# Another order of all steps in a fused attention and channel-mix kernel, batch 0's first token half first

## The chip, the cores and the metric

The kernel runs on one core of a Trainium2 chip. The metric is the device time of one execution in microseconds. All times below are microseconds unless marked ns.

The engines are called as the profile calls them: PE is TensorE (PEld its weight loads), DVE is VectorE, ACT is ScalarE, POOL is GpSimd, SP is SyncE. Each takes its own list of instructions in order and waits for semaphores that other engines or transfers raise.

## The reference

Attention over 32 memory slots for each of 8 batches and 8 heads, 576 tokens and 64 columns a head; its output, with the heads side by side, goes through a token-shifted gated channel mix of width 512 and inner width 1024.

```python
a = phi - np.max(phi, axis=2, keepdims=True)
a = np.exp(a)
a = a / (np.sum(a, axis=2, keepdims=True) + 1e-09)
k_m = np.einsum('bhsm,bhsd->bhmd', a, k)
v_m = np.einsum('bhsm,bhsd->bhmd', a, v)
scores = scale * np.matmul(q, k_m.transpose(0, 1, 3, 2))
...
attn = np.exp(scores)
attn = attn / (np.sum(attn, axis=-1, keepdims=True) + 1e-09)
return np.matmul(attn, v_m).astype(np.float32)
...
x_prev = np.concatenate([np.zeros((B, 1, D), dtype=np.float32), x[:, :-1, :]], axis=1)
xk = mu_k * x + (1.0 - mu_k) * x_prev
xr = mu_r * x + (1.0 - mu_r) * x_prev
k = np.maximum(xk @ w_k, 0.0)
v = k * k @ w_v
r = 1.0 / (1.0 + np.exp(-(xr @ w_r)))
return (r * v).astype(np.float32)
```

## The kernel before

Nothing in this kernel is scheduled by a tool at build time. `PLAN` is a table of words, and the last loop of the kernel issues the steps that the words name, one after the other. Since each engine takes its instructions in the order in which they were issued, the order of the words is the order on every engine. A word reads `who:step@banks/engine`. `who` is a batch (`0:`, `1:`), a stage of the channel mix (`c0:` keys of batch 0, `g:` gates, `o:` outputs, `r:`, `t:` and `s:` evictions of keys, of gates, and squares, `x:` left-over tokens), `p:` a load and `b:` unread matmuls. The digits behind `@` say which of the eight PSUM banks the step writes, and `/a` or `/d` whether ACT or DVE does the copy. Many steps come in two or three words: the first issues the matmuls, a later one reads their result.

The steps of a batch's attention: `exp` (L292) exponentiates phi; `kv`, `k`, `v`, `kg`, `vg` (L312) multiply it with k or v (`kvps`); `z` (L322, L326) makes the reciprocal of its sum (`rz`); `nk` or `h` (L337 on ACT, L339 on DVE) normalizes k (`kbd`); `tk` (L361, L365) transposes it (`ktps`, `kmT`); `q0` and `q1` (L381) transpose q on DVE; `s` (L395) makes the scores (`scps`); `es` (L409, L413) exponentiates them.

For batch 0, which has nothing ahead of it to hide behind, the softmax goes over two parts of the attention positions, 0 to 319 and 320 to 575: `l` (L420, L425) takes the row sum by a matmul and its logarithm, `r` (L430) the reciprocal by an exponential, `y` (L458) weighs. Then `nk0`, `nk1`, `nr0` and `nr1` (L521, `vm`) scale V by the mix factors, `mk` and `mr` (L355, `mxps`) mix tokens and values in one go, `u` (L545) unloads the mix to `x0T`, and `c0:` (L599) multiplies it with `wk`. All of these exist for tokens 0 to 255 (`mk0`, `mr0`, `c0:..a`) and 256 to 575 (`mk1`, `mr1`, `c0:..b`). The first part reads attention positions 0 to 319 alone, the second one reads positions of both parts.

For batches 1 to 7 the softmax sum is folded on DVE (`fe` L435, `fs` L441 and L442, `fo` L447) and `w` (L458) weighs. `nv` (L346, L348) normalizes V, `vt` (L463, L468) transposes it, `vm` (L473, tile `vM`) scales the transpose. `G` (L492) multiplies both into the weights, `E` (L498) copies the result, `D` (L501) takes a difference, `c1:` to `c7:` (L617, L621, L625) make the keys from it, `g:` (L679, L683, L687) the gates, and `o:` (L760 on PE, L771 on DVE) multiplies the squares with `wv` and applies the gate; then the tile is stored. The outputs of batch 0 come as two halves of the columns (`o:00a`, `o:00b`), those of the last tile, `o:71`, as pieces of 352 (`a`, stored by ACT) and 160 columns (`b`, stored by SP).

Loads of weights and of the batches stand in POOL's list; phi and k of batch 0 are loaded by ACT. A load waits on POOL for the buffer it fills, and for the eighth load ahead of it to have landed. Unread matmuls (`keep_busy`, L259) multiply a tile of zeros; nothing reads what they write. Ten of them (`WARM`) come first.

## Time and profile before

| | |
|---|---|
| three executions | 189.34, 189.7, 189.8 us; median 189.7 |
| the profiled execution, span from first to last instruction | 187.8 us; no time of its own is given beside it |
| PE, DVE, ACT, POOL busy | 181.2, 153.9, 152.0, 30.2 us |
| from 20 to 180 us | PE busy 160.0 us |
| 0 to 10, 10 to 20 us | PE busy 8.8 and 8.2 us, unread matmuls among it |
| share of the 16 DMA engines' time | 0.8 or more from 5 to 112 us |

In the profile a busy PE is not PE at its peak, since matmuls are pipelined and their ends are modelled. A row of the timeline gives the start, the time from the first start to the last end, the engine, the line, output and inputs, and the count; in brackets the idle time ahead of it and what ended that. Rows of one engine can overlap a little.

### The profile page before, as it was taken

To read this page: it belongs to the slowest core of one execution; us is meant where nothing else is said; L and a number is where in the kernel's file an instruction comes from. 1 tells how busy PE (TensorE), PEld (TensorE's weight loads), DVE (VectorE), ACT (ScalarE), POOL (GpSimd) and SP (SyncE) were. 2 spreads that over 40 slices of the span, in tenths; PEclk is the share of its full clock that TensorE was granted. 3 is DMA by queue.
4 is the path that set the end of the run, shared out by engine and by line. 5 is a ranking of instruction groups with operands and counts; after the bars stand their busy time and mean duration, and the time that the engine had idled before them with its cause. 6 is when DMAs were issued, how large, how long until landed. Compare 5 with 4: busy or idle time off the path is not lost.

```text
span 187.8 us, 6010 instructions
## 1 busy us (share of the span) xinstructions
PE 181.2 (96%) x2483; PEld 103.2 (55%) x2483; DVE 153.9 (82%) x328; ACT 151.9 (81%) x368; POOL 30.2 (16%) x46
## 2 busy tenths in 40 slices
PE   7979999999999999999999999999999999999992
PEld 2544566677644575556544655556545653465441
DVE  2334574899989999999999899999989999889441
ACT  2537889889999999999999889958999678775900
POOL 5943531060303040140032000000000010000000
PEclk9999999999999999999999999999999999999999
DMA  5999999999999999899989995114202224242054
GB/s 188 280 203 220 251 207 205 266 208 234 308 208 210 275 292 255 160 220 224 223 163 237 234 278 197 28 59 113 56 0 59 58 59 113 56 108 63 0 139 140
DMA packets 24923, 31.91 MB, mean 170 GB/s; under 512 B 1880, under 2 KB 19040, under 8 KB 24896
## 3 DMA queue, kind: packets, MB, share of 16 engines
q0 software_dynamic: 17936, 20.45, 59.0%
q1 hardware_dynamic: 5664, 9.00, 17.2%
q10 hardware_dynamic: 1296, 2.08, 3.3%
q8 instruction: 19, 0.31, 0.7%
q14 instruction: 8, 0.07, 0.1%
HBM read 38.28 MB, written 9.44 MB: 254 GB/s over the span
## 4 chain that ended last, share of the span: by engine, by line
PE 90%; DMA 4%; DVE 2%; issue 1%; ACT 1%; POOL 0%; POOLq 0%; DVEq 0%
PE pv L760 34%; PE pk L617 8%; PE pk L625 8%; PE pb L625 7%; PE gps L492 6%; PE pk L599 4%; DMA q<-in_q_dram 4%; PE pr L687 3%; PE pb L687 3%; PE pr L679 3%; PE kvps L312 3%; PE pr L709 2%; PE pr L666 2%; PE scps L395 2%; PE idle L259 1%
## 5 line engine op out<-in xcount | busy, mean ns | idle before, releaser
L760 PE MATMUL pv<-wv,sq 128*128 128x512 bf16 (+3 forms) x296 | 60.5, 350 | 0.0
L760 PEld LDWEIGHTS <-sq 128*128 128x128 bf16 x296 | 27.7, 98 | 24.9 <-issue 2.8
L498 ACT CAST G<-gps 128x512 bf16<-128x512 f32 x67 | 36.2, 629 | 1.2 <-PE gps L492 1.2
L771 DVE SCALAR_TENSOR_TENSOR o<-sg,pv 128x512 f32<-128x512 f32 (+3 forms) x41 | 24.9, 613 | 7.5 <-PE pv L760 5.1
L625 PEld LDWEIGHTS <-G 128*128 128x128 bf16 x224 | 21.4, 98 | 8.5 <-issue 0.7
L583 ACT ACTIVATE rl<-pk 128x288 bf16<-128x288 f32 (+2 forms) x49 | 20.0, 420 | 4.5 <-PE pk L625 3.9
L625 PE MATMUL pk<-diff,G 128*128 128x288 bf16 x112 | 22.9, 286 | 0.0
L625 PE MATMUL pb<-diff,G 128*128 128x288 bf16 x112 | 22.9, 286 | 0.0
L617 PE MATMUL pk<-atn,G 128*128 128x288 bf16 x112 | 20.8, 287 | 0.0
L621 ACT COPY pb<-pk 128x288 f32<-128x288 f32 x41 | 16.4, 410 | 5.1 <-PE pk L617 3.5
L591 DVE TENSOR_TENSOR sq<-rl 128x576 bf16<-128x576 bf16 (+2 forms) x46 | 18.3, 420 | 1.0 <-ACT rl L583 0.5
L583 ACT ACTIVATE rl<-pb 128x288 bf16<-128x288 f32 x40 | 16.2, 427 | 2.2 <-PE pb L625 1.8
L589 ACT ACTIVATE sq<-rl 128x576 bf16<-128x576 bf16 (+2 forms) x26 | 15.7, 624 | 0.5 <-DVE rl L585 0.4
L501 DVE TENSOR_TENSOR G<-G 128x1024 bf16<-128x1024 bf16 x21 | 14.3, 679 | 1.3 <-ACT G L498 1.3
L458 DVE TENSOR_TENSOR atn<-e,lz 128x576 bf16<-128x576 bf16 (+2 forms) x18 | 12.1, 683 | 3.5 <-ACT lz L430 3.5
L617 PEld LDWEIGHTS <-G 128*128 128x128 bf16 x112 | 10.2, 98 | 6.6 <-issue 1.5
L656 ACT ACTIVATE sg<-pr 128x512 f32<-128x512 f32 x22 | 13.0, 618 | 0.7 <-PE pr L687 0.6
L259 PE MATMUL idle<-zeros 128*128 128x512 bf16 (+3 forms) x47 | 12.2, 408 | 1.0 <-DVE zeros L187 1.0
L381 DVE STREAM_TRANSPOSE qT<-q 128x576 uint32<-128x576 uint32 (+2 forms) x16 | 12.1, 765 | 1.2 <-DMA q<-in_q_dram 1.2
L585 DVE TENSOR_SCALAR rl<-pk 128x288 bf16<-128x288 f32 (+2 forms) x23 | 10.1, 449 | 2.8 <-PE pk L599 2.6
L498 DVE CAST G<-gps 128x512 bf16<-128x512 f32 x17 | 11.3, 679 | 0.2 <-PE gps L492 0.2
L292 ACT ACTIVATE em<-ph 128x1152 bf16<-128x1152 f32 (+1 forms) x9 | 9.9, 1095 | 1.6 <-DMA ph<-in_phi_dram 1.6
(101 smaller groups left out, 283.7 us busy)
## 6 DMA issues: line engine op xcount, KB each, us to landing
out_dram<-o SPq DMA_DIRECT2D x46, 128.0 KB, 2.4
ph<-in_phi_dram POOLq DMA_DIRECT2D x7, 576.0 KB, 12.2
q<-in_q_dram POOLq DMA_DIRECT2D x7, 576.0 KB, 13.6
kv<-in_k_dram POOLq DMA_DIRECT2D x7, 576.0 KB, 14.2
kv<-in_v_dram POOLq DMA_DIRECT2D x7, 576.0 KB, 15.0
out_dram<-o SPq DMA_DIRECT2D x6, 256.0 KB, 6.5
out_dram<-o SPq DMA_DIRECT2D x20, 64.0 KB, 2.5
k0f<-in_k_dram ACTq DMA_DIRECT2D x2, 576.0 KB, 5.8
```

Of the source, the lines that this page charges most:

```text
L259: nc.tensor.matmul(ps.rearrange("p (a b) -> p a b", b=64), lhsT=zeros, rhs=zeros[:, :64].unsqueeze(1).to_broadcast([128, blocks, 64]), sta ...
L498: return lambda: copier()(g_tile()[:, v, c, GCOLS[i]], st["gps", v, i][c])
L501: return lambda: nc.vector.tensor_sub(g_tile()[:, 1, :, GCOLS[i]], g_tile()[:, 2, :, GCOLS[i]], g_tile()[:, 0, :, GCOLS[i]])
L583: nc.scalar.activation(rl, ps, AF.Relu, scale=HALF ** 0.5)
L589: nc.scalar.activation(dst, rl, AF.Square)
L591: nc.vector.tensor_mul(dst, rl, rl)
L617: nc.tensor.matmul(pa, lhsT=st["G"][:, 2, c, f], rhs=st["at"][:, c, :NP], start=c == 0, stop=False, skip_group_check=True)
L621: copier()(pb, pa)
L625: nc.tensor.matmul(ps, lhsT=st["G"][:, v, c, f], rhs=st["d"][:, kind, c], start=False, stop=c == 1, skip_group_check=True)
L656: nc.scalar.activation(gated[name], ps, AF.Tanh, scale=0.5)
L760: nc.tensor.matmul(pv[:, cols], lhsT=squares, rhs=wv_sb[:, fi, cols], start=(fi == 0), stop=(fi == NF - 1))
L771: nc.vector.scalar_tensor_tensor(o[:, cols], in0=gated[name][:, cols], scalar=1.0, in1=pv[:, cols], op0=AL.add, op1=AL.mult)
```

## The change

The table has the same steps in another order, with other banks and in part other engines for the copies. `b:` words are others too. No function changes. Of the diff, the first line of the old table and of the new one; the file is one line shorter, so each line number behind the table is lower by one in the changed kernel:

```diff
 PLAN = [
-    "p:q:0b 0:c01/d 0:exp1 p:v:0h 0:c00/a 0:exp0 b:11x6@5 0:mub@0 0:mub 0:kg0@12 0:c10/d 0:c11/a b:2x8@5 0:kg1",
...
+    "b:1x2@5 b:1x8@3 0:exp0 0:exp1 0:mub@2 0:mu@1 b:1x2@7 0:mu b:1x8@3 0:z@1 b:1x8@7 0:c01/a 0:c00/d 0:kg0@40 b:1x4@6",
...
```

**DVE in the front**, from the start of batch 0's attention to its first weighed values (`rz` reciprocal of the phi sums, `kbd` and `kmT` k for the scores, `qT` the transposed q, `atn` the weighed attention, `vm` the scaled V). Before:

```order
L297 CAST kv_72<-k0f 128x576
L381 STREAM_TRANSPOSE qT<-q_76 128x4x160
L326 RECIPROCAL rz<-zps 128x2
L365 COPY kmT<-ktps 128x256
L381 STREAM_TRANSPOSE qT<-q_77 128x4x128
L458 TENSOR_TENSOR atn<-e,lz 128x320 x2
L458 TENSOR_TENSOR atn<-e,lz 128x256
L521 SCALAR_TENSOR_TENSOR vm<-kvps,rz,mu_m 128x2x64 x2
L458 TENSOR_TENSOR atn<-e,lz 128x256
L545 CAST x0T<-mxps 128x320 x2
```

And now:

```order
L325 RECIPROCAL rz<-zps 128x2
L271 COPY mu_m<-mub 128x2x128
L272 TENSOR_SCALAR mu_m<-mub 128x2x128
L296 CAST kv_72<-k0f 128x576
L338 TENSOR_SCALAR kbd<-kvps,rz 128x2x64
L380 STREAM_TRANSPOSE qT<-q_76 128x4x160
L364 COPY kmT<-ktps 128x256
L380 STREAM_TRANSPOSE qT<-q_77 128x4x128
L457 TENSOR_TENSOR atn<-e,lz 128x320
L520 SCALAR_TENSOR_TENSOR vm<-kvps,rz,mu_m 128x2x64 x2
L457 TENSOR_TENSOR atn<-e,lz 128x320
L520 SCALAR_TENSOR_TENSOR vm<-kvps,rz,mu_m 128x2x64 x2
```

The reciprocal has moved ahead of the transposition of q, one of the two `kbd` has come to DVE from ACT, and all four `vm` stand ahead of the second part's weighing (256 wide), which follows with the first unloads, now 256 wide instead of 320. On ACT a second-part exponential pair, a logarithm and a reciprocal now alternate where the first part's four came together. On PE the order is `mk0`, `mr0`, three keys of tokens 0 to 255, `mk1`, and so on; before it was `mk1`, six keys of tokens 256 to 575, `mk0`, one more such key, `mr0`.

**POOL's list of loads**, from batch 1's q on (`kv_73` and `q_75` are buffers of the odd batches, `kv_72` and `q_74` of the even ones, `ph` is phi, `wr` and `wv` are weights). Before:

```order
L181 DMA q_75<-in_q_dram 128x4x576
L181 DMA kv_73<-in_k_dram 128x4x576
L208 DMA wr<-in_moe_w_r_dram 128x4x512
L208 DMA wv<-in_moe_w_v_dram 128x8x256
L181 DMA kv_73<-in_v_dram 128x4x576
L177 DMA ph<-in_phi_dram 128x4x288
L208 DMA wv<-in_moe_w_v_dram 128x8x256
L181 DMA kv_72<-in_v_dram 128x4x576
L181 DMA q_74<-in_q_dram 128x4x576
```

And now:

```order
L180 DMA q_75<-in_q_dram 128x4x576
L180 DMA kv_73<-in_k_dram 128x4x576
L207 DMA wr<-in_moe_w_r_dram 128x4x512
L207 DMA wv<-in_moe_w_v_dram 128x8x256
L180 DMA kv_73<-in_v_dram 128x4x576
L207 DMA wv<-in_moe_w_v_dram 128x8x256
L176 DMA ph<-in_phi_dram 128x4x288
L180 DMA q_74<-in_q_dram 128x4x576
L180 DMA kv_72<-in_v_dram 128x4x576
```

Up to batch 1's v nothing has moved, and nothing ahead of these rows either. Behind it the second half of `wv` has moved ahead of batch 2's phi, and batch 2's q ahead of its v. On PE, batch 1's V matmuls (`1:v`) now stand behind the four gates of batch 0 and two output halves (`o:00b`, `o:03b`); before, behind the four gates and one half (`o:02b`).

**DVE from batch 1's fold to its G** (`eT`, `se` and `lz` are the fold, `o` output halves of batch 0, `vM` and `vT` the transposed V that G reads). Before:

```order
L435 STREAM_TRANSPOSE eT<-e 128x576
L441 TENSOR_REDUCE se<-eT 128x36
L442 RECIPROCAL se<-se 128x36
L591 TENSOR_TENSOR sq<-rl 128x256
L447 STREAM_TRANSPOSE lz<-se 128x18x2x32
L473 TENSOR_TENSOR vM<-vtps,mu_116 128x256
L468 COPY vT<-vtps 128x128
L771 SCALAR_TENSOR_TENSOR o<-sg,pv 128x256 x3
L458 TENSOR_TENSOR atn<-e,lz 128x576 x2
```

And now:

```order
L434 STREAM_TRANSPOSE eT<-e 128x576
L440 TENSOR_REDUCE se<-eT 128x36
L441 RECIPROCAL se<-se 128x36
L446 STREAM_TRANSPOSE lz<-se 128x18x2x32
L770 SCALAR_TENSOR_TENSOR o<-sg,pv 128x256 x2
L457 TENSOR_TENSOR atn<-e,lz 128x576 x2
L472 TENSOR_TENSOR vM<-vtps,mu_116 128x256
L467 COPY vT<-vtps 128x128
L770 SCALAR_TENSOR_TENSOR o<-sg,pv 128x256 x2
```

Two output halves and both weighs have moved ahead of `vM`.

At the end of the program `o:71b` now comes ahead of `o:71a`. There are 45 unread matmuls with 20,864 columns instead of 47 with 21,376, in more and shorter groups. Over the program, DVE has nine `pb` copies (L621) fewer and ACT nine more, and five G copies (L498) have gone from ACT to DVE.

129 rows, old and new, of the table PLAN are left out of this document.

## The prediction, before the result was known

> **What bounds the kernel now.** First the page: span, busy time of the engines, and the one large group that does no work for the result.
>
> ```profile
> span 187.8 us, 6010 instructions
> PE 181.2 (96%) x2483; PEld 103.2 (55%) x2483; DVE 153.9 (82%) x328; ACT 151.9 (81%) x368; POOL 30.2 (16%) x46
> L259 PE MATMUL idle<-zeros 128*128 128x512 bf16 (+3 forms) x47 | 12.2, 408 | 1.0 <-DVE zeros L187 1.0
> ```
>
> TensorE is busy nearly throughout, but 12.2 us of that is L259, the unread matmuls, all of them ahead of the first key. Where TensorE stands still, by the list of waits (what waited, for what, us in total, times, longest); one of the longest, and the shortest:
>
> ```profile
> PE pk L599 <- DVE x0T L545: 0.5, 1, 0.5
> ...
> PE kvps L312 <- DVE kv L297: 0.2, 1, 0.2
> ```
>
> Each of these is ahead of 20 us, as the chain shows next, and the list has none later (one small gap that it does not count comes under the rivals). So the span is a front that ends at the first key matmul, a TensorE stream behind it, and a tail. A new order gains in the front; behind it there is next to nothing to gain. The chain of waits through the front:
>
> ```profile
> 10.12 0.84 DVE qT L381
> ...
> 11.06 0.63 ACT kbd L337 x2
> ...
> 12.40 0.53 PE scps L395 x30
> ...
> 14.16 1.94 PE idle L259 x9
> ...
> 18.67 0.54 PE mxps L355 x16
> ...
> 19.75 1.37 PE pk L599 x8
> ```
>
> Columns: start, us, engine and what it works for. Read it as: q is transposed, only then come kbd, scores, softmax, value mix; the first key starts at 19.75. Nine unread matmuls of 512 take 1.94, so one costs 0.216.
>
> **The front, step by step.** Rows of the timeline that price it:
>
> ```profile
> 9.01 0.44 PE L312 MATMUL kvps<-kv,em 64*32 64x64 bf16 x36 [0.17 <-DVE kv L297]
> 10.12 0.84 DVE L381 STREAM_TRANSPOSE qT<-q 128x640 uint32<-128x640 uint32 x1 [1.17 <-DMA q<-in_q_dram]
> 12.06 0.29 DVE L365 COPY kmT<-ktps 128x256 bf16<-128x256 bf16 x1 [1.04 <-PE ktps L361]
> 12.92 0.89 ACT L413 ACTIVATE e<-scps 128x160 bf16<-128x160 f32 x4 [1.24 <-PE scps L395]
> 13.80 0.83 ACT L425 ACTIVATE lz<-zps 128x320 f32<-128x320 f32 x2
> 15.02 0.89 DVE L458 TENSOR_TENSOR atn<-e,lz 128x320 bf16<-128x320 bf16 x2 [2.05 <-ACT lz L430]
> 15.08 0.88 POOL L208 DMA_DIRECT2D wv<-in_moe_w_v_dram  x1 [1.22 <-DMA kv<-in_v_dram]
> 15.24 0.77 ACT L413 ACTIVATE e<-scps 128x128 bf16<-128x128 f32 x4
> 17.68 0.60 DVE L521 SCALAR_TENSOR_TENSOR vm<-kvps,rz,mu_m 128x128 bf16<-128x128 f32 x2
> 23.22 0.42 PE L355 MATMUL mxps<-atn,vm 32*64 32x256 bf16 x16
> 23.70 0.76 DVE L545 CAST x0T<-mxps 128x256 bf16<-128x256 f32 x2
> ```
>
> *Scores.* The k loads and their casts stay, so the kvps matmuls still end near 9.01 + 0.44, with a tenth for the unread matmul now right ahead of them: 9.55. The reciprocal no longer stands behind the q transposition, and DVE and ACT make one kbd each (0.36, from the 0.63 of two) instead of ACT both: kbd is there near 9.95, not 11.69. Four unread matmuls hold TensorE to 10.3; ktps then ends near 10.6. That costs nothing, since the transposition cannot start before q lands (10.12) and covers it to 10.9. Then kmT, 0.29, and the scores start at 11.23 instead of 12.40: **1.17 earlier**. What is late next is q, a transfer that the change leaves where it is.
>
> *Softmax.* The exponentials start 0.52 behind the scores as now (12.40 to 12.92), at 11.75, and take 0.89; the first row sum and its latency bring the logarithm at 13.0. From there ACT is one queue: a logarithm of 320 goes at about 0.36 (two take 0.83, and their rows overlap), a reciprocal the same, those of 256 at 0.30, a pair of second-half exponentials at 0.31 (four take 0.77). In the new order (log, pair, log, reciprocal, pair, reciprocal, then the second half's four) the two first-half reciprocals end at 14.5 and 15.2, the last one at 17.0.
>
> *First value mix.* Its V lands just ahead of 15.08 (POOL's wait on it ends there), so its kv matmuls end near 15.3. DVE then does vm twice (0.60), the second weigh (0.41 of the 0.89), vm twice: 16.7. Here lies the point of "first token half first": tokens 0 to 255 read only attention positions 0 to 319, so the mix need not wait for the second half. Sixteen mix matmuls 0.42, two casts 0.76: the first key starts at 17.96, **1.79 earlier**. Before, 32 mix matmuls (0.54) were done by then; now two groups of 16 (0.84), another 0.3 of work ahead. Lead: 2.1.
>
> **From the first key to the values of batch 1.** What matters here is a transfer:
>
> ```profile
> 17.38 0.75 POOL L181 DMA_DIRECT2D kv<-in_v_dram  x1 [1.42 <-DMA wk<-in_moe_w_k_dram]
> DMA to landing us min/median/max: 18.1/18.1/18.1
> 29.41 0.75 PE L312 MATMUL kvps<-kv,em 64*32 64x64 bf16 x72
> 31.62 0.49 PE L395 MATMUL scps<-qT,kmT 32*32 32x288 bf16 x32
> 33.95 0.87 PE pv L760 x8
> 35.61 0.75 PE L312 MATMUL kvps<-kv,em 64*32 64x64 bf16 x72
> ```
>
> The second row is the landing of the load in the first: batch 1's V is there at 17.38 + 18.1 = 35.5, and its matmuls start at 35.61. POOL issues that load when a wk load has landed, whatever TensorE does, and POOL's list up to it is unchanged. So the new kernel cannot pass this point before about 35.55.
>
> When does it get there? From 19.75 to 35.61 TensorE needs 15.9. Now 0.3 less (mixes done), 0.87 more (two output halves stand before these matmuls instead of one), and about 1.0 of new waiting: from the end of batch 1's K matmuls (29.41 + 0.75) to its scores (31.62) pass 1.46, filled now by a gate and a key; the new order puts one key (0.44) there. 17.96 + 15.9 - 0.3 + 0.87 + 1.0 = 35.4. So TensorE arrives about when V lands, and every further tenth gained in the front would be waited away. The lead kept is the output half done earlier, 0.87, plus 0.06: **0.9**. If the hole costs nothing the arrival is 34.4 and the lead still 0.9; if it is twice as long, 36.4 and the lead 0.
>
> **Batch 1's G.** Here the change adds a wait. The first G matmuls read vM, which DVE made ahead of the output halves and the weighs; now it stands behind the fold, two output halves and two weighs.
>
> ```profile
> 33.56 0.78 DVE L435 STREAM_TRANSPOSE eT<-e 128x576 uint32<-128x576 uint32 x1 [0.96 <-ACT e L409]
> 36.20 1.37 DVE L447 STREAM_TRANSPOSE lz<-se 128x1152 f32<-128x1152 f32 x1
> 37.48 0.38 DVE L473 TENSOR_TENSOR vM<-vtps,mu 128x256 bf16<-128x256 bf16 x1
> 39.05 1.42 DVE L458 TENSOR_TENSOR atn<-e,lz 128x576 bf16<-128x576 bf16 x2
> ```
>
> The fold starts 1.94 behind the scores (31.62 to 33.56) and its last transposition 2.64 later. The new scores start four gates of four matmuls of 0.216 and two output halves (5.2) and their own 0.44 ahead of 35.4, at 29.8: fold 31.7, last transposition 34.3 to 35.7, two output halves at about 0.42 (between the 0.32 and 0.52 of the tail's rows below) to 36.5, weighs to 37.9, vM to 38.3. Rows overlap, though: 36.20 + 1.37 is 37.57, and the next starts at 37.48. Six overlaps of 0.09 bring vM to 37.8. TensorE is covered by two output halves until 35.55 + 0.75 + 1.74 = 38.0. So the wait costs between nothing and 0.3; I take nothing, with 0.2 of cover left. Queued behind a waiting G are all others of batch 1 and its keys.
>
> **What else moves.** The mu matmuls go ahead of the first exponentials, into time that unread ones fill now: nothing. Unread matmuls are 45 of 20,864 columns instead of 47 of 21,376, spread over the waits of the front; only the four ahead of ktps and the one ahead of the first key stand on a path, and both lie under something longer (the transposition, the second unload). On POOL the second wv load goes ahead of batch 2's phi, and q ahead of v: batch 2's loads come in the same total time, and the wv columns that the fifth output half reads come sooner. SP's stores follow the tiles' new order; nothing but the end waits for SP.
>
> **Behind that.** The same matmuls follow. Lists of DVE and ACT swap work (nine half-key copies to ACT, five G casts to DVE), which leaves both about as full. The price of the new order there lies between -0.3 (the one gap of the stream goes, below) and +1.6 (one such gap in each of six batches). I take 0, nearest to the rows in which TensorE never waits.
>
> **The tail.** Of the last tile the 352 wide piece now comes last, instead of the 160 wide one.
>
> ```profile
> L771 DVE SCALAR_TENSOR_TENSOR o<-sg,pv 128x352 f32<-128x352 f32 x1 | 0.5, 521 | 0.6 <-PE pv L760 0.6
> L771 DVE SCALAR_TENSOR_TENSOR o<-sg,pv 128x160 f32<-128x160 f32 x1 | 0.3, 320 | 0.0
> out_dram<-o ACTq DMA_DIRECT2D x1, 176.0 KB, 2.3
> out_dram<-o SPq DMA_DIRECT2D x1, 80.0 KB, 2.3
> ```
>
> 0.521 - 0.320 = **0.2 later**; both stores land after 2.3.
>
> **Sum**, against the profiled execution: 187.8 - 0.9 + 0.0 + 0.2 = 187.1. The three times (median 189.7) lie about 1.9 above that span; taking 1.9 as unchanged gives **189.0**.
>
> **The rivals.**
>
> *The clock.* The sparsest stretch of the front, and one of the stream behind it:
>
> ```profile
> 10.00:13.40 3.40, 2.43 (x74) 1.11 (x73) 1.81 (x4) 1.11 (x5) 1.76 (x3) 1.00 1.24 206
> 60.00:80.00 20.00, 20.00 (x326) 11.66 (x325) 19.57 (x37) 19.94 (x53) 2.98 (x4) 1.00 1.08 243
> ```
>
> TensorE is busy 2.43 of 3.40 there and the granted clock stays 1.00. If the clock halved there in executions that were not profiled, the change would save more: the matmuls on the chain above between 12.40 and 19.75 come to 0.53 + 1.94 + 0.54 = 3.0, which at half speed cost as much again, so up to 3.0 more: 186.0. Against it: the three times lie within 0.46. [...]
>
> *The front's lead is kept whole.* If V lands sooner, 1.6 to 2.0 remain: 188.0 to 188.4. Against it stands POOL's unchanged list.
>
> *The change does not do what it says.* If the hole in batch 1's scores, or the table load and casts on ACT among the keys, eat a second us more, the lead is 0: 187.8 + 0.2, so 189.9.
>
> *Slower: G casts on DVE.* Two rows of the chain, each 16 matmuls of G:
>
> ```profile
> 76.70 0.84 PE gps L492 x16
> ...
> 98.13 0.57 PE gps L492 x16
> ```
>
> The first one is longer by 0.27, most likely for a bank that was not yet emptied. DVE is busy 19.57 of 20 in that stretch, and the new order gives it five more G casts. Such a gap in each of batches 2 to 7 is 1.6, so 190.6; from five of them on (1.35 on top of 189.0) the result is slower than before by more than 0.3%, 190.3. For it: DVE has no slack there. Against it: DVE gives away nine copies, and only one gap of this kind is in the trace now.
>
> **How the numbers follow.** Forecast (lead 0.9, tail 0.2) 0.50, own range 188.6 to 189.5; lead kept whole 0.12; clock 0.04; lead lost 0.18, at 189.9; gaps on G 0.16, 190.3 to 190.6. A difference of 0.3% (0.57 us) is about what a measurement of this kernel can tell from none. Two thirds of the forecast's range are faster by more than that: 0.33 + 0.12 + 0.04 = 0.49 faster; the rest of it with the lost lead, 0.35, the same; 0.16 slower. The range 188.2 to 190.4 leaves out the clock, the faster end of the lead kept whole and most of the gaps on G.
>
> **What would show it.** Right: first key near 18.0; V of batch 1 landing at 35.5 with TensorE waiting for it there at most a few tenths to 1 us; two output halves ahead of it; last DVE instruction 352 wide and 0.52 long. Wrong: a first key later than 19; V's matmuls well behind 35.6; waits of TensorE on G banks behind 60 us; a granted clock below 1.00.

## The result, and the profile after

The changed kernel takes **191.8 us** (median of four executions: 190.9, 191.5, 192.0, 192.3) against 189.5 for the kernel before: ratio **1.0115**, 95% interval 1.0094 to 1.0135. It is slower, and it spreads over 1.5 us where the kernel before spreads over 0.5. One execution of a later kernel, `code_alone`, fell into a slower state of the chip and is left out of its time and ratio. The profiled execution is the fastest of the four, 190.9 with a span of 189.1. Its page:

```profile
span 189.1 us, 6003 instructions
PE 180.3 (95%) x2461; PEld 102.5 (54%) x2481; DVE 156.2 (83%) x335; ACT 149.3 (79%) x361; POOL 30.1 (16%) x46
q8 instruction: 19, 0.31, 0.6%
L258 PE MATMUL idle<-zeros 128*128 128x512 bf16 (+2 forms) x45 | 12.9, 408 | 1.2 <-DVE zeros L186 1.0
```

Engines and unread matmuls look as before (20 matmul records are missing in this trace). The third line will matter: 19 packets of 0.31 MB in all, 16 KB each, by a queue that carries instructions. The timeline of TensorE through the front:

```profile
14.94 0.95 PE L311 MATMUL kvps<-kv,em 64*32 64x64 bf16 x72
...
16.27 1.14 PE L258 MATMUL idle<-zeros 128*128 128x512 bf16 x5
17.33 0.42 PE L354 MATMUL mxps<-atn,vm 32*64 32x256 bf16 x16
...
18.93 1.47 PE L598 MATMUL pk<-x0T,wk 128*128 128x256 bf16 x12
20.33 0.48 PE L354 MATMUL mxps<-atn,vm 32*64 32x256 bf16 x32
20.75 0.28 PE L598 MATMUL pk<-x0T,wk 128*128 128x256 bf16 x1
21.61 1.06 PE L598 MATMUL pk<-x0T,wk 128*128 128x256 bf16 x8 [0.58 <-issue]
...
34.47 1.91 PE L759 MATMUL pv<-wv,sq 128*128 128x256 bf16 x16
36.31 0.75 PE L311 MATMUL kvps<-kv,em 64*32 64x64 bf16 x72
```

The first key starts at 18.93 instead of 19.75, so the front does lead, by 0.8. Then, after a single matmul of a key, TensorE stops for 0.86 (20.75 to 21.61) and the releaser reads "issue": no semaphore that the profile shows. (A stop is given here from the start of one matmul to the start of the next, where the trace has a pause; the idle time in brackets, 0.58, is less, since ends are modelled.) Batch 0's V matmuls (14.94) take 0.95 where 72 of them took 0.75 before. And the matmuls of batch 1's V start at 36.31; the load they read landed at 35.3.

Two places further on. At 97 us, and the last output pieces on DVE and ACT:

```profile
97.06 0.59 PE L686 MATMUL pb<-G,diff 128*128 128x512 bf16 x2
97.80 0.90 PE L311 MATMUL kvps<-kv,em 64*32 64x128 bf16 x72 [0.15 <-DMA kv<-in_v_dram]
```

```profile
183.07 0.69 DVE L770 SCALAR_TENSOR_TENSOR o<-sg,pv 128x512 f32<-128x512 f32 x1 [0.98 <-PE pv L759]
185.04 0.75 DVE L770 SCALAR_TENSOR_TENSOR o<-sg,pv 128x160 f32<-128x160 f32 x2 [1.28 <-DMA out_dram<-o]
...
183.79 0.57 ACTq L744 DMA_DIRECT2D out_dram<-o  x1
184.41 0.60 ACT L655 ACTIVATE sg<-pb 128x512 f32<-128x512 f32 x1 [4.28 <-DVE o L770]
```

TensorE now waits for batch 5's V: two matmuls of 0.216 from 97.06 end at 97.49, the next start at 97.80, 0.31 lost. At the end DVE stands still from 183.76 to 185.04. The profile puts that down to a store that landed, but the piece starts 0.03 behind the end of the sigmoid in the last row (184.41 + 0.60), and that sigmoid stood on ACT behind the issue of a store, which itself waits for the output tile that DVE finishes at 183.76. In the new table the sigmoid's word (`t:701`) comes behind `o:72`; in the old one it came two tiles earlier.

### The profile page after: what moved, and what is told of

Its sections match the earlier page's. It is cut to its first block, busy times and chain, and to the rows that moved or that the text cites. A ratio compares the mean times of both kernels' runs of the same rounds, so it can differ in the third digit from the quotient of the medians.

```text
span 189.1 us, 6003 instructions
## 1 busy us (share of the span) xinstructions
PE 180.3 (95%) x2461; PEld 102.5 (54%) x2481; DVE 156.2 (83%) x335; ACT 149.3 (79%) x361; POOL 30.1 (16%) x46
## 4 chain that ended last, share of the span: by engine, by line
PE 79%; DMA 11%; DVE 3%; issue 2%; ACT 1%; POOL 1%; SPq 1%; DVEq 0%; POOLq 0%
PE pv L759 28%; DMA kv<-in_v_dram 8%; PE pk L616 7%; PE pk L624 6%; PE pb L624 6%; PE gps L491 5%; PE kvps L311 4%; PE pk L598 4%; PE idle L258 3%; PE pb L686 3%; PE pr L686 3%; PE pr L678 2%; DMA ph<-in_phi_dram 2%; PE pr L665 2%; PE scps L394 2%
## 5 line engine op out<-in xcount | busy, mean ns | idle before, releaser
L497 ACT CAST G<-gps 128x512 bf16<-128x512 f32 x62 | 33.3, 623 | 2.2 <-PE gps L491 2.2
L620 ACT COPY pb<-pk 128x288 f32<-128x288 f32 x50 | 19.6, 415 | 4.3 <-PE pk L616 1.4
L590 DVE TENSOR_TENSOR sq<-rl 128x576 bf16<-128x576 bf16 (+2 forms) x51 | 20.3, 418 | 1.0 <-ACT rl L582 0.5
L616 PE MATMUL pk<-atn,G 128*128 128x288 bf16 x112 | 19.4, 286 | 0.1
L582 ACT ACTIVATE rl<-pb 128x288 bf16<-128x288 f32 x42 | 17.3, 431 | 0.8 <-PE pb L624 0.6
L655 ACT ACTIVATE sg<-pb 128x512 f32<-128x512 f32 x14 | 9.0, 646 | 8.1 <-DVE o L770 4.3
L497 DVE CAST G<-gps 128x512 bf16<-128x512 f32 x22 | 14.4, 682 | 0.2 <-PE gps L491 0.2
L258 PE MATMUL idle<-zeros 128*128 128x512 bf16 (+2 forms) x45 | 12.9, 408 | 1.2 <-DVE zeros L186 1.0
L588 ACT ACTIVATE sq<-rl 128x576 bf16<-128x576 bf16 (+2 forms) x21 | 12.9, 623 | 0.9 <-DVE rl L584 0.6
L408 ACT ACTIVATE e<-scps 128x288 bf16<-128x288 f32 x28 | 9.3, 428 | 2.1 <-PE scps L394 2.0
```

What stands on the lines that cost most here:

```text
L258: nc.tensor.matmul(ps.rearrange("p (a b) -> p a b", b=64), lhsT=zeros, rhs=zeros[:, :64].unsqueeze(1).to_broadcast([128, blocks, 64]), sta ...
L497: return lambda: copier()(g_tile()[:, v, c, GCOLS[i]], st["gps", v, i][c])
L582: nc.scalar.activation(rl, ps, AF.Relu, scale=HALF ** 0.5)
L588: nc.scalar.activation(dst, rl, AF.Square)
L590: nc.vector.tensor_mul(dst, rl, rl)
L616: nc.tensor.matmul(pa, lhsT=st["G"][:, 2, c, f], rhs=st["at"][:, c, :NP], start=c == 0, stop=False, skip_group_check=True)
```

## The experiments

Three explanations were on the table: losses in several places (front, stream, tail), the front alone, or the granted clock.

### Four cuts through the change

**One word of the tail.**

```diff
-g:e3@7 o:e3@0 o:e3 o:72@5 o:72 o:71b@4 t:701 o:71b o:71a@2 o:71a
+t:701 g:e3@7 o:e3@0 o:e3 o:72@5 o:72 o:71b@4 o:71b o:71a@2 o:71a
```

> The changed kernel with one word moved: the sigmoid of the last tile's gate (ACT, L655) is issued ahead of the fifth tile of left-over tokens, as in the kernel before, so that it no longer stands on ACT behind the issue of a store. Theory (three pieces: front, stream and tail each give a part): the last two output pieces wait in the changed kernel for that sigmoid (184.41 to 185.0), 0.40 longer than for TensorE; so 0.4 off, the changed kernel's 191.8 becomes 191.4, last DVE piece right behind the last matmul. Rival (the wait is on the output buffers, as the list of releasers has it, DMA out_dram<-o): nothing changes, 191.8, and DVE still waits 1.3 ahead of the 160 wide piece.

190.9 (nine executions, 190.0 to 192.8), ratio 1.0075 (1.0042 to 1.0108): 0.9 off by the medians, where 0.4 was expected, though the spread is wider than that and the interval overlaps that of the changed kernel. DVE no longer waits. Four executions lie at 190.0 to 190.1, the others up to 2.7 above. The profiled one is 190.9, and its timeline shows why it isn't faster:

```profile
14.90 0.41 PE L311 MATMUL kvps<-kv,em 64*32 64x64 bf16 x32
16.48 0.48 PE L311 MATMUL kvps<-kv,em 64*32 64x64 bf16 x40 [1.17 <-issue]
```

In the midst of batch 0's V matmuls TensorE stops for 1.36, again for "issue". Their input landed at 13.9.

**Half of the table from each kernel.** `front_before` has the old words up to batch 1's G and then the new order of what is left; `rest_before` the new words up to the first `c1:` and then the old order.

> The front of the kernel before (all words up to the first two keys of batch 1), then the changed kernel's order of all that is left, its tail included. Theory (three pieces): the front of the changed kernel is 0.2 behind the one before at the first keys of batch 1, so 0.2 off, 191.5. Rival A (the front carries the whole loss): the loss is gone but for the tail's 0.65, about 190.2. Rival B (unread matmuls scattered over the front let the granted clock fall in some executions, spans up to 190.6 at 0.996 to 0.999): the clock is 1.000 in all executions and the spread of 1.5 us shrinks to the 0.5 of the kernel before, 191.0 or less.

> The changed kernel's front up to the first keys of batch 1, then the order of the kernel before for all that is left, its tail included. Theory (three pieces): 0.3 of the stream and 0.65 of the tail are gone and 0.2 of the front stays, so 189.5 + 0.2 to 0.4, 189.7 to 189.9. Rival A (the front carries the loss): 191 or more. Rival B (clock): executions with a clock below 1.000 and a spread over 1 us stay.

192.8, ratio 1.0179 (1.0163 to 1.0195), and 192.5, ratio 1.0150 (1.0119 to 1.0181). Both missed. The first is slower than either kernel, the second no better than the changed one, so these cuts don't divide the loss: the seam makes waits of its own. In `front_before` a key of batch 1 waits 0.6 for a copy of G on ACT. In `rest_before` a key of batch 1 waits for an output half on DVE that empties its bank, and that half stands on DVE behind two G casts and the difference of G (TensorE's row, then DVE's):

```profile
42.31 1.05 PE L759 MATMUL pv<-wv,sq 128*128 128x256 bf16 x8
45.06 0.41 PE L616 MATMUL pk<-atn,G 128*128 128x288 bf16 x2 [1.70 <-DVE o L770]
```

```profile
42.79 1.28 DVE L497 CAST G<-gps 128x512 bf16<-128x512 f32 x2
...
43.99 0.69 DVE L500 TENSOR_TENSOR G<-G 128x1024 bf16<-128x1024 bf16 x1
...
44.59 0.42 DVE L770 SCALAR_TENSOR_TENSOR o<-sg,pv 128x256 f32<-128x256 f32 x1
```

What `rest_before` does show: with the same front as the changed kernel, the stops in V and behind the first keys are there again (1.28 and 0.57), while `front_before` has neither.

**Fewer unread matmuls.** Those that end later than the operand of what follows them:

```diff
-0:h0/d b:2x8@6 b:1x8@6 b:1x8@3 0:h1/a
+0:h0/d 0:h1/a
-0:y00 b:2x8@5 b:1x4@2 p:v:0h
+0:y00 p:v:0h
-b:1x4@0 0:r11 0:y11 b:2x8@3 0:mk0@2061 b:1x8@3 0:uk01/d b:1x8@7 0:r01 0:y01 0:uk00/a 0:mr0@4573 b:1x8@2
+0:r11 0:y11 b:1x8@3 0:mk0@2061 0:uk01/d 0:r01 0:y01 0:uk00/a 0:mr0@4573
```

> The changed kernel without eleven of the unread matmuls of its front (four of 512 ahead of the transposition of k, three ahead of batch 0's V, four of 256 or 512 around the first mixes and the first key), which in the trace end later than the operand of what follows them. Theory (they stand on the path): scores near 11.3 instead of 11.66, first key at 18.0 to 18.4 instead of 18.93, and since batch 1's V lands at 35.1, 1.2 ahead of its matmuls, the end moves too: 0.5 to 0.9 off, 190.9 to 191.3. Rival A (a vector or scalar engine is late anyway): first key at 18.8 to 18.9, no change. Rival B (the clock falls when TensorE is idle there): clock below 1.000, 192 or more.

190.9, ratio 1.0068 (1.0055 to 1.0081). Two of seven executions ran at a mean clock of 0.991 and 0.988 and took 192.3 and 192.7; the other five, at 0.998 to 1.000, took 190.7 to 190.9. The profiled one is among the two. Stretches of it (start and end, length, busy time of PE, PEld, DVE, ACT and POOL with counts, PEclk, DMA), and one of the changed kernel:

```profile
10.00:14.00 4.00, 2.75 (x109) 1.36 (x103) 1.90 (x4) 1.74 (x7) 2.23 (x3) 1.00 1.24 205
14.00:19.00 5.00, 3.17 (x80) 1.66 (x78) 2.02 (x6) 2.79 (x10) 1.84 (x3) 0.74 1.33 228
```

```profile
14.00:19.00 5.00, 4.88 (x121) 2.35 (x120) 3.52 (x11) 4.07 (x14) 2.05 (x3) 1.00 1.34 231
```

With TensorE busy 63% of five microseconds the granted clock fell to 0.74; at 98% it stayed. So thinning out the unread matmuls seems to cost some executions the clock, and them 1.7. That is not separated from a stop of 1.75 in the same five microseconds (16.78 in the table below), although `tail_gate` kept its clock through one of 1.36. What the thinning does to the first key can't be read from this trace, with its low clock; the five executions at full clock lie 0.9 below the median of the changed kernel, at the upper end of the 0.5 to 0.9 expected.

### What stops TensorE for "issue"

The stops are at the same place in another sense too. Numbering TensorE's instructions from the start (each matmul is two, its weight load and itself), they lie behind instruction **449** in three kernels with that front and in `fewer_unread`, and behind **705**: 256 apart. The packets of the instruction queue fit that: the changed kernel has 2481 weight loads, so 4962 TensorE instructions, and among them the 194th and each 256th behind it are 19 places; its page counts 19 packets, of 16 KB each. That one packet is the code of one such block is read from these counts and from the times below. Worked out from the trace's records of each instruction and packet (us; "load" is the packet that starts next):

```text
                   enters 194th; load          enters 450th (stop); load        enters 706th (stop)
before               9.23; 12.76 to 13.72        16.55 (0.02); 19.81 to 20.71     24.00 (0.00)
changed              9.68; 13.18 to 14.13        15.40 (0.25); 19.27 to 20.23     21.61 (0.86)
tail_gate            9.64; 14.14 to 15.09        16.48 (1.36); 20.11 to 21.06     22.41 (0.58)
rest_before          9.52; 13.93 to 14.83        16.26 (1.28); 19.85 to 20.75     22.18 (0.57)
fewer_unread        10.04; 14.50 to 15.46        16.78 (1.75); 20.37 to 21.26     24.33 (0.00)
```

Each load starts 3.3 to 4.5 behind the entry into a block, takes 0.9 to 1.0, and where TensorE is stopped it goes on 1.3 to 1.4 behind the load's end. Where TensorE was stopped, 5.7 to 6.8 had passed since the entry before. The kernel before takes 7.3 and 7.5 over these two blocks; the new front would take 5.5 and 5.4. That is an explanation after the fact, so it was made to predict stops.

**The entries moved.** More instructions ahead move the entries to other places of the program. `early_code` has 80 more in the changed kernel, `before_late_block` 192 more in the kernel before, and `before_control` 64 more.

```diff
 early_code
-WARM = (10, 8)
+WARM = (6, 8)
-    "b:1x2@5 b:1x8@3 0:exp0
+    "b:45x1@5 b:1x8@3 0:exp0
 before_late_block (before_control: 45x1, WARM 8)
-WARM = (10, 8)
+WARM = (4, 8)
-0:exp0 b:11x6@5 0:mub@0
+0:exp0 b:113x1@5 0:mub@0
```

> The kernel before with 96 more TensorE matmuls (192 instructions) early: its eleven unread matmuls of 384 become 113 of 64, and the warm-up goes from ten to four. Theory (code): the entries into blocks then fall on what were instructions 257 (12.4 us) and 513 (16.8 us), 4.4 us apart, under the 5.8 that a load takes: TensorE stops 1.4 us or more at what was instruction 513, among batch 0's unread matmuls behind its V or its first mix, first key at 21.1 or later instead of 19.75, and the kernel is slower, 190.9 to 192. Rival (code is not the cause): within 0.3 of the kernel before, 189.5.

191.3, ratio 1.0110 (1.0092 to 1.0127). The stop is where the theory put it, in a kernel that had none:

```profile
16.01 0.63 PE L309 MATMUL kvps<-kv,em 64*32 64x64 bf16 x58
18.26 0.29 PE L309 MATMUL kvps<-kv,em 64*32 64x64 bf16 x14 [1.62 <-issue]
```

It is behind instruction 705 again, now within batch 0's V: entry into the block ahead at 12.07, load 15.80 to 16.69, on at 18.26, a stop of 1.81. It fell a little earlier than foreseen, within V and not behind it, so the first key is at 20.67 where 21.1 or later was expected; and there is a second stop of 0.81 at 31 us, at the next entry but one. The time grew by 1.9.

> The kernel before with 32 more matmuls (64 instructions) early, made in the same way: eleven of 384 become 45 of 64, the warm-up goes from ten to eight. Theory (code): the entries fall on what were instructions 129, 385 and 641, 6.3 and 6.4 apart, just above what a load takes, and nothing changes: 189.5, at most 0.5 more where a load starts late. Rival (more early instructions or shorter unread matmuls cost time or clock by themselves): slower by as much as a third of what before_late_block loses.

190.1, ratio 1.0033 (1.0022 to 1.0045): 0.6 more, above what was foreseen. No stop in the front, as expected, but one of 0.55 at 55 us, at a later entry. By the time alone the rival can't be turned down: a third of what `before_late_block` loses is 0.6 too. What speaks for the code is where the stops are, at entries in both.

> The changed kernel with its first unread matmul of 128 columns replaced by 45 of 64, and the ten of 512 that warm TensorE up cut to six: 80 more TensorE instructions in all, ahead of the first use of data. Theory (code): TensorE's code comes in blocks of 256 instructions (16 KB each in the trace), the load of the next block starts 3.5 to 4.5 us after TensorE enters a block and TensorE can go on about 2.3 us after that; so two entries lie at least 5.8 us apart. In the changed kernel the entries (instructions 449 and 705) are 5.7 and 6.2 apart with gaps of 0.25 and 0.86 in which TensorE waits for no semaphore. With 80 instructions more ahead, the entries move to what was instruction 369 and 625, 6.1 and 8.7 apart in the old trace, so both gaps go, about 1.1 us in the best executions and 2 in the others: 189.7 to 190.0 instead of 191.8, and a smaller spread. Rival (the gaps come from transfers or from waits that the profile does not show, bound to the place in the program): they stay at the second half of batch 0's V matmuls and behind the first key of column block 0, and the time stays at 191.8 or grows by the added work.

191.2, ratio 1.0098 (1.0083 to 1.0113): 0.6 off by the medians, 0.3 by the ratios, whose intervals overlap, where 1.8 to 2.1 were expected. So a gain is not shown. The front did what the theory says:

```profile
14.88 0.75 PE L311 MATMUL kvps<-kv,em 64*32 64x64 bf16 x72
...
33.68 1.91 PE L759 MATMUL pv<-wv,sq 128*128 128x256 bf16 x16
35.52 0.75 PE L311 MATMUL kvps<-kv,em 64*32 64x64 bf16 x72
```

V runs through in 0.75, the stop behind the first keys is 0.21, and batch 1's V matmuls start at 35.52 with two output halves done. But the stream has tight places too, and one of them now falls on an entry; and what was gained up to there waits for a transfer:

```profile
53.50 0.62 PE L491 MATMUL gps<-wk,vT 64*32 64x512 bf16 x14
54.72 0.39 PE L491 MATMUL gps<-wk,vT 64*32 64x512 bf16 x2 [0.60 <-issue]
...
97.13 0.59 PE L686 MATMUL pb<-G,diff 128*128 128x512 bf16 x2
98.23 0.59 PE L311 MATMUL kvps<-kv,em 64*32 64x128 bf16 x47 [0.50 <-DMA kv<-in_v_dram]
```

A stop of 0.97 at 54 us, and 0.67 at 97 instead of 0.31.

**The same with the tail** as in the kernel before (sigmoid, and the 352 wide piece first):

> The same, and in the tail the sigmoid of the last tile ahead of the left-over tokens' tile (as in the run tail_gate), and the 352 wide piece of the last tile ahead of the 160 wide one, as in the kernel before. Theory: early_code less 0.4 to 0.8 (sigmoid) less 0.2 (piece order), 188.8 to 189.2, so at or below the kernel before. Rival (code is not the cause): 190.9 less 0.2, 190.7.

191.3, ratio 1.0104 (1.0076 to 1.0132), 190.6 to 192.6. The profiled span is 188.8 where `early_code` had 189.4, but the medians don't differ: the spread swallows the tail.

### The tail and the transfer, one by one

In the kernel before, which spreads little, each part of the tail can be had alone.

```diff
 before_gate
-o:73 t:701 o:e3 o:72@2 o:72 o:71a@0 o:71a o:71b@4 o:71b
+o:73 o:e3 o:72@2 o:72 t:701 o:71a@0 o:71a o:71b@4 o:71b
 before_order
-o:71a@0 o:71a o:71b@4 o:71b
+o:71b@4 o:71b o:71a@0 o:71a
```

> The kernel before with one word moved the other way: the sigmoid of the last tile's gate is issued behind the sixth-last output tile's store, on ACT behind the issue of that store, as the changed kernel has it. Theory (in the tail the sigmoid waits in ACT's queue behind the store's issue): in the kernel before ACT issues that store from 183.2 to 183.8, so the sigmoid ends at 184.4 and the 352 wide piece starts at 184.45 instead of 183.76: 0.5 to 0.7 slower, 190.0 to 190.2. Rival (the last pieces wait for output buffers): no change, 189.5.

189.9, ratio 1.0022 (1.0010 to 1.0034), 0.4 slower, a little less than expected. The last piece pair and ACT ahead of it:

```profile
184.46 0.75 DVE L768 SCALAR_TENSOR_TENSOR o<-sg,pv 128x352 f32<-128x352 f32 x2 [1.27 <-DMA out_dram<-o]
...
183.22 0.57 ACTq L742 DMA_DIRECT2D out_dram<-o  x1
183.83 0.60 ACT L653 ACTIVATE sg<-pb 128x512 f32<-128x512 f32 x1 [5.96 <-DVE o L768]
```

The same picture as in the changed kernel, made by moving one word. The pieces start at 184.46, 0.03 behind the sigmoid, instead of 183.76; the list again names a store.

> The kernel before with the 160 wide piece of the last tile ahead of the 352 wide one. Theory (as predicted): 0.2 slower, 189.7. Rival (the two stores come closer together or further apart and decide it): a change of 0 or of over 0.5.

189.7, ratio 1.0012 (1.0004 to 1.0021): 0.23, as predicted.

**The transfer at 97 us.**

```diff
-p:q:5 p:q:6 p:k:5 p:v:6 p:v:5 p:phi:7
+p:q:5 p:k:5 p:v:5 p:q:6 p:v:6 p:phi:7
```

> The run early_code with one more change on POOL: of the loads of batches 5 and 6, k and v of batch 5 go ahead of q of batch 6, whose buffer is not free before 80 us. Theory (transfer): in the changed kernel and in early_code TensorE waits at 97 us for batch 5's V, which lands at 97.8 and 98.2 since its load stands on POOL behind that q; so 0.5 to 0.9 off, 190.3 to 190.7, with no wait of TensorE for a transfer near 97. Rival (another wait takes its place at once, such as G on its casts): 191.2.

191.4, ratio 1.0086 (1.0067 to 1.0104). The wait is gone,

```profile
98.05 0.59 PE L686 MATMUL pb<-G,diff 128*128 128x512 bf16 x2
98.57 0.80 PE L311 MATMUL kvps<-kv,em 64*32 64x128 bf16 x72
```

and the load that these matmuls read is issued at 70.2 instead of 82.6 and lands at 86.6. Yet the time isn't better: in this profiled execution the front is 0.7 later than in `early_code` (first key 19.39, not 18.67), and the stop at 54 us is still there, 1.04. The 0.7 is there before any code stop: batch 0's second K matmuls start at 10.20, not 9.48. What the front loses differs from one execution to the next by more than the wait is worth.

### Do they add up?

**All repairs.** `all_three` takes four warm-up matmuls away (8 instructions), besides tail and loads. `code_alone` and `code_tail_loads` put 126 short unread matmuls ahead of the warm-up, so that no entry falls on the place at 54 us:

```diff
+    def short_ones(n):
...
+            nc.tensor.matmul(pair[c][g * 32:(g + 1) * 32, :64], lhsT=zeros[ROWS[c], :32], rhs=zeros[ROWS[c], :64],
+                             start=True, stop=True, skip_group_check=True)
...
-WARM = (10, 8)
+WARM = (7, 8)
+    short_ones(126)
     keep_busy(*WARM)
```

> The changed kernel with the three repairs: four warm-up matmuls (8 instructions) fewer, so that the entries into code blocks fall on what were instructions 457 and 713; sigmoid and piece order in the tail as in the kernel before; loads as in early_code_loads. Theory: second gap in the front (0.86) down to 0.4 or less, first gap as it was (0.25, or 1.3 where a load starts late), 0.5 at 97 us, 0.8 in the tail: best executions 188.9 to 189.2, median 189.6 to 190.2. Rival (the order itself is slower in the stream): 190.7 or more.

> The changed kernel with 126 short unread matmuls (64 rows by 32 weights, as the kernel's own small ones) ahead of its warm-up and seven instead of ten of 512 behind them: 246 TensorE instructions more, so the entries into code blocks fall on what were instructions 203, 459 and 715, and the later ones 10 further on than in the changed kernel. Nothing else is changed. Theory (code): the gap at the first key block (0.86) goes, the one in V stays at 0.3, none at 54 us; TensorE then meets batch 5's V, which lands at 97.8, 0.5 to 0.9 earlier and waits there. Since a part of the lead is waited away, 0.6 to 1.2 off: 190.6 to 191.1. Rival (code gaps cost nothing at the end since other waits lie behind them): 191.8. Rival (short matmuls let the clock fall): clock below 0.995, over 191.8.

> The same with the sigmoid and the piece order of the tail as in the kernel before, and batch 5's k and v ahead of batch 6's q on POOL. Theory: the changed kernel without its four losses (code, transfer at 97 us, sigmoid, piece order) is 187.1 to 187.5 in its span, as forecast, 189.0 to 189.4 in time; a spread of 1 us by late code loads stays. Rival (the new order has a further loss in the stream): 190 or more.

191.9, 192.5 and 191.2 (ratios 1.0135, 1.0163, 1.0085). All missed. All three change the warm-up, and the profiles of the first two show a slower TensorE early on. Three of six executions of `all_three` ran at a clock of 0.986 to 0.988. Its profiled one is not among them, yet its trace has no record of the granted clock before 10.25 (in the other eighteen the first record starts at 3.9 to 6.6). Until then unread matmuls of 512 columns start 0.43 apart, not 0.216, and the eight ahead of batch 0's second K matmuls take 2.84, where the changed kernel takes 1.85 for them:

```profile
7.98 2.84 PE L258 MATMUL idle<-zeros 128*128 128x256 bf16 x8
10.76 0.45 PE L311 MATMUL kvps<-kv,em 64*32 64x64 bf16 x36
```

In the profile of `code_alone` the clock falls early:

```profile
7.00:11.00 4.00, 2.60 (x42) 1.25 (x42) 1.83 (x5) 1.34 (x2) 2.03 (x4) 0.70 1.30 204
```

In `code_tail_loads` the place at 54 us is clean, but a load of code starts 4.45 behind its entry (10.10, load from 14.55), and V stops for 1.26. Its rival, a further loss in the new order (190 or more), has the time right; how much of one there is, is worked out from `tail_loads` at the end.

**Without touching the front**: the changed kernel with tail and loads repaired, its code stops left as they are; and last `early_code_tail` with the loads.

> The changed kernel with the sigmoid, the piece order and batch 5's loads as in code_tail_loads, and its early instructions as they are (ten warm-up matmuls). Theory: the code gaps of the front stay (0.25 + 0.86, or 1.3 + 0.6 where a load of code starts late), the rest of the losses goes: 0.4 to 0.8 (sigmoid), 0.2 (piece), up to 0.5 (transfer): 190.2 to 190.9, best executions 189.2 to 189.5. Rival (these losses are not the causes, the front alone is): 191.5 or more.

190.6 (190.1 to 191.3), ratio 1.0065 (1.0045 to 1.0085): **1.1 off**, in the middle of the range expected. The stops in its front are 0.26 and 0.85, as in the changed kernel, and DVE's last two pieces follow at once:

```profile
21.11 0.28 PE L598 MATMUL pk<-x0T,wk 128*128 128x256 bf16 x1
21.97 0.70 PE L598 MATMUL pk<-x0T,wk 128*128 128x256 bf16 x5 [0.58 <-issue]
```

```profile
184.30 0.88 DVE L770 SCALAR_TENSOR_TENSOR o<-sg,pv 128x352 f32<-128x352 f32 x2 [0.51 <-PE pv L759]
```

> early_code_tail (191.3, best 190.6) with batch 5's loads moved too. Theory: no code gap in the front, one of 1.0 at 54 us, no wait at 97: 190.2 to 190.8, best 189.7 to 190.0. Rival (another wait takes the place of the transfer): 191.2.

191.2, ratio 1.0090 (1.0067 to 1.0112): missed. In its profiled execution the first load starts 4.5 behind its entry and the entry into the 450th instruction stops for 1.0, the next for 0.5, and the place at 54 us for 1.04.

**And the kernel before**, 24 instructions later in its blocks (`b:11x6@5` becomes `b:23x3@5`):

> The kernel before with twelve more early matmuls (24 instructions; eleven of 384 become 23 of 192). Theory (code): in the trace of the kernel before, its entries into code blocks are at least 5.8 apart but for one pair (5.5, ending at 29.7); 24 instructions later in the program that pair goes too, so nothing to 0.3 off, 189.2 to 189.5. Rival (any change of the early instructions costs, as in before_control): 189.7 to 190.1.

189.7, ratio 1.0002 (0.9987 to 1.0018): no change. No variant of the new order came under the kernel before.

## Why the prediction was wrong

Forecast was a span of 187.1, measured are 189.1 in the profiled execution, which is the fastest of the four. By its own steps:

- **The front.** The scores were to start at 11.23, they start at 11.66. The lateness begins at the K matmuls ahead of them, which were to end at 9.55 and end at 9.98. Their cast ends later (9.21, not 8.96 as in the kernel before), and eight unread matmuls, costed at a tenth of a microsecond, hold TensorE 0.3 longer. Then kbd, the transposition of q (10.32, not 10.12) and that of k follow:

```profile
8.46 0.75 DVE L296 CAST kv<-k0f 128x576 bf16<-128x576 f32 x1 [0.61 <-DMA k0f<-in_k_dram]
```

```profile
7.75 1.85 PE L258 MATMUL idle<-zeros 128*128 128x256 bf16 x8
9.53 0.45 PE L311 MATMUL kvps<-kv,em 64*32 64x64 bf16 x36
...
11.66 0.37 PE L394 MATMUL scps<-qT,kmT 32*32 32x160 bf16 x32 [0.39 <-DVE kmT L364]
```

In the seven traces with the old front these K matmuls start at 8.6 to 9.3, in the twelve with the new one at 9.4 or later, each time right behind the unread ones. First key: forecast 17.96, measured 18.93. Of the 0.97, 0.25 is the stop in V, and about 0.7 are unread matmuls costed at nothing: five that end at 17.33 when the second weighing had ended at 16.96, and three with the second mix between the first mix and the first key.
- **The lead at batch 1's V.** Forecast was an arrival of TensorE at 35.4 and a lead of 0.9. Measured is 36.31. Without the two stops (0.25 + 0.86) it is 35.2, at a landing of 35.3; and in `early_code`, where they are gone, the matmuls start at 35.52 with one output half of 0.87 more behind them than before, at 35.61: a lead of 0.96. But that the arrival came out is luck. The first key was 0.7 late even without the stop in V, and the 1.0 of new waiting at batch 1's scores did not come: from the first key to V pass 17.38, 16.5 without the stop of 0.86, which is 15.9 - 0.3 + 0.87 with nothing for the hole. The two errors cancel.
- **The step that failed is a term that is missing: the stops for code.** "Sum" went from the front's work to its time with nothing between them but waits for operands and banks; that TensorE's code arrives in blocks, and that a front which runs through one in less than 5.7 us is stopped, isn't in it, nor among the rivals. The two stops are 1.11 in the profiled execution. The lead is 0.87 + 35.61 - 36.31 = 0.17, not 0.9, so 0.73 of it is lost. (Not all of the 1.11: V landed at 35.3, and without the stops TensorE would have waited there for a tenth and been 0.3 ahead of the forecast.) `tail_gate` and `rest_before` have the same front, and stopped for 1.94 and 1.85 where the first load started 0.9 later; that the slower executions of the changed kernel are such ones is likely, not shown, since only the fastest was profiled.
- **vM and G.** Bounded at 0 to 0.3; TensorE waits 0.17 ahead of the first G (8 matmuls from 37.93 end at 38.80, G starts at 38.97). Right.
- **Behind that: -0.3 to +1.6, taken 0.** 0.31 by the transfer at 97 us. The text says of POOL's list behind batch 1 only that loads come in the same total time. It didn't look at batches 5 and 6, where the new order puts k and v of batch 5 behind q of batch 6, which has to wait for its buffer. The rival on G casts did not come true.
- **The tail, +0.2.** The piece order was right (0.23 alone). The sigmoid behind ACT's store issue was missed: the prediction listed where words moved on DVE and the pieces, not that `t:701` passed an issue that waits. The profiled execution loses 0.40 by it: the last matmul starts at 184.46 and ends at 184.78, a piece follows the last matmul by about 0.1, and the 352 wide one starts at 185.27. Alone it costs 0.4 (`before_gate`).

The sum: 187.1 + 0.73 (stops) + 0.17 (vM) + 0.31 (transfer) + 0.40 (sigmoid) = 188.7, of 189.1. In `early_code`, where the stops in the front are all but gone, the median is better by only 0.3 to 0.6, since the stop at 54 us and a longer wait at 97 us take the rest; so that the stops cost 0.73 at the end is worked out from one trace, not shown by taking them away. The last matmuls of the kernel before and of the changed one show where the other 0.4 lies:

```profile
181.66 2.56 PE L760 MATMUL pv<-wv,sq 128*128 128x512 bf16 x19
```

```profile
181.79 2.99 PE L759 MATMUL pv<-wv,sq 128*128 128x512 bf16 x21
```

TensorE ends at 184.22 before and at 184.78 now, 0.56 later, where a lead of 0.17 and waits of 0.17 and 0.31 make 0.31: 0.25 of the stream is not placed. From there to the span's end pass 3.58 and 4.32, 0.74 more, where the order of pieces and the sigmoid make 0.6. The other 0.14 is two things that nearly cancel. The last store lands sooner behind its piece, and SyncE, which at the program's end (L847) waits for the semaphores of the stores one by one in a fixed order, has more waits left when it has landed. In the kernel before the last store to land is the last in that order; in the changed kernel seven more waits of 0.06 come behind it. From the traces' records (us):

```text
              last piece ends   its landing seen   waits left   span's end
before        184.58            186.93             0            187.82
changed       185.79            187.77             7            189.09
tail_gate     186.17            188.23             0            189.11
tail_loads    185.17            187.48             7            188.81
```

That is one execution, the fastest. The median lies 0.9 above it, and what the slower ones lose is open. `tail_loads` takes 1.1 off the median of the changed kernel and leaves it 1.2 above the kernel before. Its profiled execution (span 188.8, 1.0 above) shows what is left. Batch 1's V starts at 36.67, so with an output half more behind it the new front with its stops is 0.2 behind the old one. From V to the end of the last matmul 148.14 pass where 148.61 - 0.87 = 147.74 would do: 0.4, of which 0.17 is vM and 0.23 is not placed. Behind the last matmul it is 0.4 again: the pieces are as before, SyncE's seven waits are not. A gain from the shorter front is not shown by any variant.

The clock as a rival was given 0.04, beside the row of the kernel before at 2.43 of 3.40 busy. That was right for that kernel (1.00 there), but such a row tells little of others: at 3.17 of 5.00 in `fewer_unread` and 2.60 of 4.00 in `code_alone` the clock fell to 0.74 and 0.70. In `fewer_unread` most of the idle time is one stop of 1.75; what lowers the clock is not shown. The 3.0 behind the 186.0 is half speed from 12.40 to 19.75, and no run shows that: by estimate it would leave a mean clock of 0.98 (half of 7.35 us in 187.8), and the lowest mean of an execution is 0.996 in the kernel before and 0.985 in all runs (`code_alone`). Half speed is seen in the kernel before at its start: unread matmuls of 512 columns stand 0.43 apart up to 4.81, and 0.216 later.

## What to carry to other kernels

Before work is packed closer on TensorE, number its instructions and look how long each 256 of them take: here many small matmuls (72 pairs in 0.75) brought two blocks of the front down to 5.5 and 5.4 us, TensorE went on only 5.7 and 6.2 behind the entries ahead, the profile said "issue" at the longer stop, and changes that put more instructions ahead brought stops elsewhere (0.97 at 54 us in `early_code`, 0.55 at 55 us in `before_control`). Treat the issue of a store on a computing engine as an instruction that waits, and list what is queued behind it (here a sigmoid, 0.4 alone in `before_gate`); where a releaser looks odd, compare the start with the ends of everything else that the instruction reads. When a front gets shorter, go down the loads of the whole kernel for the next one that lands too late, and cost unread matmuls as work: they stand on the path of what comes behind them as soon as its operand is there first (here 0.3 ahead of the scores and about 0.7 ahead of the first key).

## What the runs showed that was not expected

- **Code.** In the front every block of 256 TensorE instructions that would have been run through in less than 5.7 us ended in a stop, and one of 5.9 stopped for 1.0 where the load was late (`early_code_tail_loads`): the load of the next starts from 3.3 behind the entry (kernel before) to 4.5 (`tail_gate`), takes 0.9 to 1.0, and 1.3 to 1.6 pass from its end until TensorE goes on (1.6 in `before_late_block`). Stops of 0.2 (`early_code`) to 2.1 us (`all_three`) were seen. Further on in the stream the load's start varies more, from 4.5 behind the entry (`fewer_unread`, at 69 us) to 1.3 ahead of it (kernel before, 95.58 for an entry at 96.88). What sets it is open. The kernel before passes the two entries of its front with 0.02 and 0.00 of stop; the new front loses 0.25 and 0.86 at them.
- **Early instructions move the time.** 64 more early instructions put 0.6 on the kernel before, 192 more put 1.9 on it, and 24 more nothing; 80 more took at most 0.6 off the changed kernel, which is not clear of its spread.
- **The spread.** Executions of one kernel at a clock of 1.000 differ by up to 2.8 us (`tail_gate`), by 0.5 to 1.4 within a series of the kernel before. The start of a code load that varies by 1 us accounts for about 0.8 of it (stops of 1.94 in `tail_gate`, 1.11 in the changed kernel). The records point at a second source, not tried: the first record of the granted clock starts at 3.9 to 6.6 us, 10.25 once, and a clock of 1.000 doesn't tell of what is ahead of it. In the new front the second K matmuls, bound to the unread ones ahead of them, start at 9.36 where that record starts at 3.88 (`rest_before`) and at 10.20 where it starts at 6.62 (`early_code_loads`). The rest stays open.
